# Seven quarter products for eight in one block product of a blocked token mixer

## The chip, the core and the metric

The kernel runs on one core of a Trainium2 chip. A core has five engines with queues of their own: TensorE (PE in the profile, its weight loads PEld), VectorE (DVE), ScalarE (ACT), GpSimd (POOL) and SyncE (SP), which mostly issues transfers. The metric is the device time of one execution in microseconds. Lower is better.

## The reference, cut to what matters

```python
x = x + A(layernorm(x), wqkv, wo)                        # 32 heads of 18, a query sees 8 keys, 2 apart
x = x + B(layernorm(x), w_in, w_sp, b_sp, w_out)
x = x + A(...); x = x + B(...)                           # the same weights again

def B(x, w_in, w_sp, b_sp, w_out):                       # S=2048 tokens, D=576, Fh=2304
    z = gelu(x @ w_in)                                   # 2048 x 4608
    z1, z2 = z[:, :Fh], layernorm(z[:, Fh:])
    g = w_sp @ z2 + b_sp[:, None]                        # 2048 x 2048 times 2048 x 2304
    return (z1 * g) @ w_out
```

The change concerns `w_sp @ z2`, the largest product of the program. It is computed twice, once for each B.

## The kernel before

The program has five phases: an attention stage (`phase_F(0)`, which also computes z2), a mixing stage (`phase_S(1)`), the same two again (`phase_F(2)`, `phase_S(3)`), and a last stage with the product by `w_out` (`phase_E`). In the attention stages a planner (`Flow`) orders the steps of all engines ahead of time. Each step has a cost, a key, the steps that it comes after and the buffers that it holds; the planner plays the engines forward and writes the instructions in the order that comes out. A step's cost on POOL or SP therefore takes part in the order of everything behind it. The constants of this play are in `PLANS`. `SIDE` names the queue of the stage's side transfers: POOL at 0.66 us in the first attention stage, SP in the second. `win2.0` to `win2.9` load a part of `w_in` on it, each after the logits step `a3.L` to `a12.L` of a tile of queries.

In a mixing stage the order is written out by hand. The stage has 18 units: nine feature tiles `jj` (each 2 x 128 features, s = 0 and 1) for each half `c` of the 2048 target tokens, numbered n = 0 to 17, the first half first. A unit multiplies 2 x 128 features by 2048 source tokens and 1024 target tokens. The operands are split in two in each dimension: z2 into B[b, s] (source half b, feature half s), w_sp into A11, A12, A21 and A22 (target block, source half). The product of two such 2 x 2 block matrices is taken with seven block products and sums for the usual eight:

- `A11`: B[0,0] with A11, into PSUM bank y
- `A12`: B[1,0] with A12, into bank x
- `S1`, `S2`, `S4`, `S3`: B or the sums T1 to T3 with S1 to S4, sums of the blocks of w_sp, into banks v and y
- `A22`: T4 with A22, into bank y

Each is eight matmuls of 128 x 128 by 128 x 512 (`eight`, L1281). Bank y alternates between two banks from unit to unit; x and v are one bank each. After each group VectorE evicts the bank (`plus`, L1303: scale, add the bias or an earlier part) into one of three buffers g0 to g2 and multiplies finished blocks by z1 (`times_u`, L1293). For A12 that is an eviction that adds g0, and a product. The T sums of the next unit (`t_op`, L1289) are made as soon as the present unit has used theirs. Between S3 and the end the unit also takes the z1 product of the next unit (`z1_a`, `z1_b`, 20 matmuls, L1254 and L1262), which ScalarE evicts with the GELU (L1266).

The sums of w_sp for the first half are made at the end of the first attention stage, and those for the second half in the first mixing stage: a transposing DMA brings a piece, ScalarE scales it (L1417), VectorE makes its sums (L1424), POOL stores it. That goes on beside units 2 to 7, at places named in a table. In unit 8 the blocks of the second half are loaded over those of the first. In the second mixing stage both halves come from DRAM.

The query, key and value weights lie in SBUF for the whole program in five tiles: `wqk`, `wqk_r` and `wqk_e` (query and key, in an order that the first stage makes with VectorE, POOL and ScalarE copies), `wv` and `wv_r` (value). Both attention stages read them, no mixing stage does.

Of the kernel before, what the change touches and what calls it, by code (L numbers as in the profile page):

```python
# [46 lines left out]
ORDER = ("A11", "A12", "S1", "S2", "S4", "S3", "A22")  # L47
PLACED = ("A11", "A12", "S1", "S2", "S4", "S3", "A22")
BLOCKS = ("A11", "A12", "A22", "S3", "S1", "S2", "S4")

# [218 lines left out]
class K:  # L269
# [17 lines left out]
    def setup(self):  # L287
        nc, tc, ctx = self.nc, self.tc, self.ctx
        c = self.base = ctx.enter_context(tc.tile_pool(name="base", bufs=1))
        self.dram = ctx.enter_context(tc.tile_pool(name="dram", bufs=1, space=DRAM))  # L290
        self.xres = [self.dram.tile([S, D], bf16, name=f"xres{i}") for i in range(2)]
        self.psum = ctx.enter_context(tc.tile_pool(name="ps", bufs=1, space=PSUM)).tile([P, 8, 512], f32, name="psum")
        self.flow, self.turn, self.pair_at = None, [0, 0], (0, 1, 2, 3)
        self.xnD = c.tile([P, NM + 1, 2080], bf16, name="xnD")[:, :, 16 - PADL:16 - PADL + XW]
        self.ident = c.tile([P, P], bf16, name="ident")
        self.maskT = c.tile([P, QH], bf16, name="maskT")
        self.mask0 = c.tile([P, QH], bf16, name="mask0")
        self.zu = c.tile([P, NZ, 2 * S], bf16, name="zu")
        self.wA = c.tile([P, WA * 2, D], bf16, name="wA")
        self.wqk = c.tile([P, NM, NM, 2, P], bf16, name="wqk")  # L300
        self.wqk_r = c.tile([P, NM, P], bf16, name="wqk_r")
        self.wqk_e = c.tile([P, NM + 1, P], bf16, name="wqk_e")
        self.wv = c.tile([P, NM, 2, 2, 144], bf16, name="wv")
        self.wv_r = c.tile([P, 2, 2, 144], bf16, name="wv_r")
        self.wsc = c.tile([P, 8], f32, name="wsc")
        self.neg_half = self.wsc[:, 7:8]
        self.ustore = [self.dram.tile([P, S], bf16, name=f"ustore{j}") for j in range(NB)]
        self.ops = {(k, n): self.dram.tile([P, 8 * 512], f16 if n[0] == "S" else bf16, name=f"op{k}_{n}")
                    for k in range(1) for n in BLOCKS}
        self.ops1 = self.dram.tile([P, len(BLOCKS), 8 * 512], bf16, name="op1")  # L310
        self.first_pairs, self.blk = None, {}
        make_identity(nc, self.ident[:])
        self.idle = self.zu[:, NB, 0:512]
        nc.vector.memset(self.idle, 0.0)
        nc.vector.memset(self.neg_half, -0.5)
        self.xn_writes, self.xn_strided = [], []
        self.wrote_xn(nc.vector.memset(self.xnD[:, :, 0:PADL], 0.0), 0, PADL)
        self.wrote_xn(nc.vector.memset(self.xnD[:, :, PADL + S:XW], 0.0), PADL + S, XW)
# [212 lines left out]
    def phase_F(self, li):  # L531
# [550 lines left out]
        for i in range(NS):  # L1082
            Z2_steps(i, pl.KZ + pl.KS * i, [f"win2.{k}" for k in range(len(win2_parts()))] +
                     ([] if first else [f"p3_{j}.m11" for j in range(NS)]))
        fl.step("blocks", "SP", 0.0, 900, lambda _: self.open_blocks(li + 1, acm), [f"w{i}.m1" for i in range(NS)])
        (self.make_ops if first else self.load_first_ops)(fl)
        self.flow = fl
# [113 lines left out]
    def phase_S(self, li):  # L1201
# [27 lines left out]
        def bias(c, a):  # L1229
            return bsp[:, b_of[c, a], :]  # L1230
# [48 lines left out]
        def eight(ps, lhs, rhs, opens):  # L1279
            for i in range(8):  # L1280
                nc.tensor.matmul(ps, lhsT=lhs[:, i, :], rhs=rhs[:, i, :], start=(opens and i == 0), stop=(i == 7),  # L1281
                                 skip_group_check=not opens)
            self.pairs += 8

        def t_op(jj, k):

            B = z_of(jj)
            a, b = {1: (B[0, 1], B[0, 0]), 2: (B[1, 1], T[0][:]), 3: (B[1, 1], B[0, 1]), 4: (B[1, 0], T[1][:])}[k]
            nc.vector.tensor_tensor(out=T[k - 1][:], in0=a, in1=b, op=ALU.subtract)  # L1289

        def times_u(u, a, s, g):
            uv = u[:, s, 512 * a:512 * a + 512]
            nc.vector.tensor_tensor(out=uv, in0=g, in1=uv, op=ALU.mult)  # L1293

        def unit(n, jj, c, z1, t_next, at):
            B, u = z_of(jj), u_of(jj, c)
            y = self.psum[:, Y.start + n % 2, :]
            x, v = self.psum[:, XV.start, :], self.psum[:, XV.start + 1, :]
            g0, g1, g2 = (t[:] for t in tmp)
            h0, h1, h2 = (t[:].bitcast(bf16)[:, 0:512] for t in tmp)  # L1300

            def plus(out, ps, other):
                nc.vector.scalar_tensor_tensor(out=out, in0=ps, scalar=inv[c], in1=other, op0=ALU.mult, op1=ALU.add)  # L1303

            def t_one(k):
                if t_next is not None:
                    t_op(t_next, k)
            at("begin")
            eight(y, B[0, 0], A["A11"], True)
            at("A11")  # L1310
            plus(g0, y, bias(c, 0))
            at("first")
            eight(x, B[1, 0], A["A12"], True)
            at("A12")
            plus(h1, x, g0)
            times_u(u, 0, 0, h1)
            eight(v, T[0], A["S1"], True)
            at("S1")
            plus(g1, v, bias(c, 1))
            at("third")  # L1320
            t_one(1)
            eight(y, T[1], A["S2"], False)
            at("S2")
            plus(g2, y, bias(c, 0))
            t_one(2)
            eight(v, B[1, 1], A["S4"], False)
            at("S4")
            plus(h0, v, g2)
            times_u(u, 0, 1, h0)
            eight(y, T[2], A["S3"], False)  # L1330
            at("S3")
            plus(h2, y, g1)
            times_u(u, 1, 1, h2)
            if z1:
                z1_a(*z1, ZB)
            t_one(3)
            at("second")
            eight(y, T[3], A["A22"], False)
            at("A22")
            plus(h0, y, bias(c, 1))  # L1340
            times_u(u, 1, 0, h0)
            t_one(4)
            if z1:
                z1_b(*z1, ZB)
            at("end")
# [87 lines left out]
                piece_load(i + 2)  # L1433

        seq = [(jj, c) for c in range(2) for jj in range(NB)]
        for n, (jj, c) in enumerate(seq):
            nxt = seq[n + 1] if n + 1 < len(seq) else None
            z1 = nxt
            if n + 2 < len(seq):
                load_w1(*seq[n + 2])  # L1440

            def at(where, n=n, jj=jj, c=c):
                if first and n < 2:
                    first_sums(n, where)
                for part, k in pieces.get((n, where), ()):
                    if part == 0:
                        piece_scale(k)
                    else:
                        piece_sums(k, part - 1)
                    if part == 2:  # L1450
                        piece_store(k)
                if where == "S3":
# [16 lines left out]
            unit(n, jj, c, z1, nxt[0] if nxt else None, at)  # L1469
            if c == 0:  # L1470
                spill(jj)
        order.__exit__(None, None, None)
# [86 lines left out]
```

## Time and profile before

| | |
|---|---|
| median of 3 runs | 1132.14 us (1129.98 to 1133.3) |
| profiled execution | 1129.72 us, its span 1128.0 us |
| granted TensorE clock | 0.997 |
| busy share of the span | PE 98%, DVE 63%, ACT 38%, POOL 19% |
| first mixing stage, first z1 matmul | 201.9 us |
| first matmul of unit 0, of unit 1 | 206.0 and 229.2 us |
| second attention stage, first matmul | 500.1 us |
| second mixing stage, first z1 matmul | 761.8 us |
| last stage | about 1052 to 1128 us |

The profile is of one execution, 2.4 us below the median of the runs. Times count from the start of the span. A row names engine, line, operation, output and inputs, shape and number, then the time busy and the mean of one; behind the bar or in brackets stands how long the engine was idle before, and what ended that. Matmuls are pipelined, so the mean of one (381 ns for 512 columns) is its latency and not the spacing of two.

### The profile page before, as it was taken

The numbers are of one execution on the slowest core, as the hardware profiler recorded it, in microseconds if no ns is written. First come the engines' busy times: TensorE is split into PE (matmuls) and PEld (weight loads), VectorE is DVE, ScalarE is ACT, GpSimd is POOL, SyncE is SP. The second block draws the span as 40 slices with busy tenths as digits, with TensorE's granted clock in tenths as the row PEclk, the third lists the DMA queues.
The fourth block names the chain that finished last, engine by engine and source line by source line (L and its number), as shares of the span: only waits on it lengthen the run. The fifth ranks groups of instructions, "written<-read, shape, count | busy, mean of one in ns | idle before, by whom it ended". The sixth has DMA issues, their size and how long they took to land. (4 is left out here: it accounts for less than half of the span.)

```text
span 1128.0 us, 24364 instructions
## 1 busy us (share of the span) xinstructions
PE 1103.6 (98%) x10109; PEld 612.2 (54%) x10147; DVE 712.4 (63%) x1205; ACT 431.2 (38%) x684; POOL 217.3 (19%) x436
## 2 busy tenths in 40 slices
PE   8999999899999999999999999999999999999998
PEld 5777655344444444457777765554444444444676
DVE  8898888866765555554566777556555555555311
ACT  7788897642221101103454668772101110111000
POOL 6353538302110000022111214520000000000000
PEclk9999999999999999999999999999999999999999
DMA  7866460658967331133444777602112383221221
GB/s 191 166 141 134 104 138 1 176 165 243 247 215 283 117 117 42 46 108 95 73 70 73 122 164 185 203 1 56 49 40 59 85 311 88 72 56 38 85 64 53
DMA packets 187528, 131.82 MB, mean 117 GB/s; under 512 B 145273, under 2 KB 171769, under 8 KB 183833
## 3 DMA queue, kind: packets, MB, share of 16 engines
q1 hardware_dynamic: 179032, 96.54, 35.2%
q0 software_dynamic: 8384, 33.72, 9.2%
q8 instruction: 79, 1.29, 0.5%
q14 instruction: 33, 0.26, 0.1%
HBM read 68.40 MB, written 31.20 MB: 88 GB/s over the span
## 5 line engine op out<-in xcount | busy, mean ns | idle before, releaser
L1266 ACT ACTIVATE zu<-psum 128x1024 bf16<-128x1024 f32 x72 | 73.5, 1023 | 436.3 <-PE psum L1262 386.9
L1303 DVE SCALAR_TENSOR_TENSOR g<-psum,wsc,bsp 128x512 f32<-128x512 f32 (+1 forms) x144 | 108.0, 750 | 154.2 <-PE psum L1281 153.8
L1281 PE MATMUL psum<-S,T 128*128 128x512 f16 x864 | 199.9, 381 | 0.2 <-DVE T L1289 0.2
L1281 PEld LDWEIGHTS <-T 128*128 128x128 f16 x1152 | 113.0, 98 | 138.9 <-issue 4.3
L1281 PEld LDWEIGHTS <-zu 128*128 128x128 bf16 x864 | 84.5, 98 | 107.8 <-DVE zu L964 3.8
L1254 PE MATMUL psum<-xnD,w 128*128 128x512 bf16 x540 | 134.5, 380 | 1.9
L1281 PE MATMUL psum<-A,zu 128*128 128x512 bf16 x576 | 130.7, 379 | 2.7 <-DVE zu L964 2.7
L481 PEld LDWEIGHTS <-zu 128*128 128x128 bf16 x1152 | 112.5, 98 | 29.3 <-issue 0.2
L1303 DVE SCALAR_TENSOR_TENSOR g<-psum,wsc,g 128x512 bf16<-128x512 f32 x108 | 81.1, 751 | 62.5 <-PE psum L1281 62.1
L900 PE MATMUL psum<-wA,xnD 128*128 128x384 bf16 x576 | 109.7, 327 | 0.3 <-DVE v_ext L461 0.3
L481 PE MATMUL psum<-wA,zu 128*128 128x288 bf16 x768 | 105.0, 286 | 0.0
L900 PEld LDWEIGHTS <-xnD 128*128 128x128 bf16 x768 | 72.0, 98 | 56.2 <-issue 12.2
L1254 PEld LDWEIGHTS <-w 128*128 128x128 bf16 x576 | 53.4, 98 | 74.3 <-issue 15.3
L923 ACT ACTIVATE zu<-psum 128x768 bf16<-128x768 f32 x96 | 76.8, 804 | 22.7 <-PE psum L907 17.4
L933 DVE CUSTOM_DVE_ANT_1 zu<-zu 128x1536 bf16<-128x1536 bf16 x32 | 56.0, 1751 | 29.1 <-ACT zu L923 28.8
L1281 PE MATMUL psum<-S,zu 128*128 128x512 f16 x288 | 68.0, 379 | 2.1 <-DVE g L1303 2.1
L1281 PE MATMUL psum<-A,T 128*128 128x512 bf16 x286 | 67.9, 379 | 1.5 <-DVE g L1303 1.4
L786 ACT ACTIVATE P<-psum 128x912 bf16<-128x912 f32 x72 | 64.0, 944 | 9.5 <-PE psum L779 7.7
L1293 DVE TENSOR_TENSOR zu<-g,zu 128x512 bf16<-128x512 bf16 x144 | 61.2, 425 | 10.0 <-DVE g L1303 0.9
L391 PE MATMUL psum<-xnD,wqk 128*128 128x228 bf16 (+1 forms) x480 | 64.9, 280 | 2.4 <-ACT xnD L462 1.2
L391 PEld LDWEIGHTS <-wqk 128*128 128x128 bf16 x480 | 43.8, 97 | 16.9 <-issue 7.6
L427 ACT ACTIVATE xn<-xt,ln_st 128x512 bf16<-128x512 bf16 x72 | 42.9, 647 | 20.4 <-POOL ln_st L414 20.3
(151 smaller groups left out, 1336.3 us busy)
## 6 DMA issues: line engine op xcount, KB each, us to landing
w<-in_B_w_in_dram SPq DMA_DIRECT2D x72, 128.0 KB
ustore<-zu POOLq DMA_DIRECT2D x18, 512.0 KB, 3.6
zu<-ustore SPq DMA_DIRECT2D x18, 512.0 KB
S<-op SPq DMA_DIRECT2D x8, 1024.0 KB
A<-op SPq DMA_DIRECT2D x6, 1024.0 KB
QK<-stg SPq DMA_DIRECT2D x36, 114.0 KB
QK<-stg SPq DMA_DIRECT2D x24, 171.0 KB
wA<-in_B_w_sp_dram POOLq DMA_DIRECT2D x8, 512.0 KB, 4.8
```

The costliest lines, as they stand in the source:

```text
L391: nc.tensor.matmul(ps(s), lhsT=lhsT, rhs=rhs, start=(c == 0 and not rest_first), stop=(c == NM - 1 and rest_first))
L427: nc.scalar.activation(out=out, in_=in_, func=ACT.Identity, scale=rstd[:n], bias=nmr[:n])
L481: nc.tensor.matmul(ps[:, hh, 0:288], lhsT=u[:, s * S + i * P:s * S + (i + 1) * P], rhs=wout(b, s)[:, hh * 288:(hh + 1) * 288], start=(b == ...
L786: nc.scalar.activation(out=Psb[:, 2 * hh:2 * hh + 2, :, 0:QH], in_=box["L", hh][:, :, 0:8 * QH].rearrange("p a (b c) -> p a b c", c=QH), f ...
L900: nc.tensor.matmul(box[u][:, s, 0:384], lhsT=self.xnD[:, c, at], rhs=(win2a[:, c, s] if c < NM - 1 else win2b[:, s])[:, cols], start=(firs ...
L923: nc.scalar.activation(out=self.zu[:, 3 * u:3 * u + 3, 256 * i:256 * (i + 1)].rearrange("p j (s r) -> p s j r", s=2), in_=box[u][:, :, 0:3 ...
L933: nc.vector.tensor_tensor_reduce(out=junk(0, 6), in0=z[:, 0:6, :], in1=z[:, 0:6, :], scale=1.0 / FH, scalar=0.0, op0=ALU.mult, op1=ALU.add ...
L1254: nc.tensor.matmul(ps[:, h, :], lhsT=w1[:, NM * h + d, :], rhs=self.xnD[:, d, t0:t0 + 512], start=(opens and d == 0), stop=(not opens and ...
L1266: nc.scalar.activation(out=u_of(jj, c)[:, :, 512 * k:512 * k + 512], in_=ps, func=ACT.Gelu_apprx_tanh)
L1281: nc.tensor.matmul(ps, lhsT=lhs[:, i, :], rhs=rhs[:, i, :], start=(opens and i == 0), stop=(i == 7), skip_group_check=not opens)
L1293: nc.vector.tensor_tensor(out=uv, in0=g, in1=uv, op=ALU.mult)
L1303: nc.vector.scalar_tensor_tensor(out=out, in0=ps, scalar=inv[c], in1=other, op0=ALU.mult, op1=ALU.add)
```

## The change

Units 2 and 3, 4 and 5, 6 and 7 of the first half, and the tiles 0 and 1, 2 and 3, 4 and 5, 6 and 7 of the second, form pairs. For a pair the product of B[1,0] with A12 is taken for both tiles together, in the first unit of the pair (kind "two"). Seen as one product it has 2 x 128 features (one 128 from each tile), 1024 source tokens and 512 target tokens, and is again split in two in each dimension: seven quarter products of four matmuls of 128 x 128 by 128 x 256 (`four`), where two times eight matmuls of 512 columns stood. The part that belongs to the second tile is kept in f32 (`late`), and the second unit (kind "parked") has no A12 group: it adds `late` to its A11 and multiplies by z1 at once. Tile 8 of each half and units 0 and 1 (kind "one") stay as they were.

The sums that the quarters need are SQ (four of 128 x 1024, from A12, made once for each half by `s_quarter`) and TQ (four of 128 x 512, from the z2 of both tiles, made by `t_quarter` in the unit before the pair, between S3 and A22). SQ, TQ, `late` and the finished block `hq` lie in the space of the query, key and value weights, which become one tile `wqkv` with five parts. In the first attention stage four stores on POOL's queue (`keep0` to `keep3`, after the logits of tiles 13 to 16) copy it to DRAM, and at the start of unit 17 of the first mixing stage one load on SP's queue brings it back. After the second attention stage it is not needed any more.

```diff
+WQ = (0, 4096, 4608, 5248, 7552, 8128)
...
+        self.wqkv = c.tile([P, WQ[-1]], bf16, name="wqkv")
+        part = [self.wqkv[:, WQ[k]:WQ[k + 1]] for k in range(5)]
...
+        self.wqkv_d = self.dram.tile([P, WQ[-1]], bf16, name="wqkv_d")
...
+            for k in range(4):
+                fl.step(f"keep{k}", *SIDE, 0, lambda _, k=k: self.dma(self.wqkv_d[:, 2032 * k:2032 * k + 2032], self.wqkv[:, 2032 * k:2032 * k + 2032], side),
+                        made + [f"a{13 + k}.L"])
...
+        def s_quarter(k):
+            to, x, y, op = ((SQ[0], quarter(1, 0), quarter(1, 1), ALU.add), (SQ[2], quarter(0, 0), quarter(1, 0), ALU.subtract),
+                            (SQ[1], SQ[0], quarter(0, 0), ALU.subtract), (SQ[3], quarter(0, 1), SQ[1], ALU.subtract))[k]
+            nc.vector.tensor_tensor(out=to, in0=x, in1=y, op=op)
...
+        def t_quarter(jj):
+            B = z_quarters(jj)
+            for k, a, b in ((0, B[0, 1], B[0, 0]), (1, B[1, 1], TQ[0]), (2, B[1, 1], B[0, 1]), (3, B[1, 0], TQ[1])):
+                nc.vector.tensor_tensor(out=TQ[k], in0=a, in1=b, op=ALU.subtract)
+
+        def four(ps, lhs, rhs, opens):
+            for i in range(4):
+                nc.tensor.matmul(ps, lhsT=lhs[:, i, :], rhs=rhs[:, i, :], start=(opens and i == 0), stop=(i == 3),
+                                 skip_group_check=not opens)
...
             at("A11")
-            plus(g0, y, bias(c, 0))
+            if kind == "parked":
+                plus(h1, y, late)
+                times_u(u, 0, 0, h1)
+            else:
+                plus(g0, y, bias(c, 0))
             at("first")
-            eight(x, B[1, 0], A["A12"], True)
+            if kind == "one":
+                eight(x, B[1, 0], A["A12"], True)
+            if kind == "two":
+                four(yq, Q[0, 0], quarter(0, 0), True)
             at("A12")
...
+            if kind == "two":
+                plus(g0[:, half(0)], yq, g0[:, half(0)])
             eight(v, T[0], A["S1"], True)
             at("S1")
             plus(g1, v, bias(c, 1))
             at("third")
             t_one(1)
+            if kind == "two":
+                four(xq, Q[1, 0], quarter(0, 1), True)
+                plus(hq[:, half(0)], xq, g0[:, half(0)])
             eight(y, T[1], A["S2"], False)
             at("S2")
             plus(g2, y, bias(c, 0))
             t_one(2)
+            if kind == "two":
+                four(xq, TQ[0], SQ[0], True)
+                plus(late[:, half(1)], xq, bias(c, 0)[:, half(1)])
+                four(yq, TQ[1], SQ[1], False)
+                plus(late[:, half(0)], yq, bias(c, 0)[:, half(0)])
             eight(v, B[1, 1], A["S4"], False)
             at("S4")
             plus(h0, v, g2)
             times_u(u, 0, 1, h0)
+            if kind == "two":
+                four(xq, Q[1, 1], SQ[3], False)
+                plus(late[:, half(0)], xq, late[:, half(0)])
+                four(yq, TQ[2], SQ[2], False)
+                plus(late[:, half(1)], yq, late[:, half(1)])
             eight(y, T[2], A["S3"], False)
             at("S3")
             plus(h2, y, g1)
             times_u(u, 1, 1, h2)
+            if kind == "two":
+                four(yq, TQ[3], quarter(1, 1), False)
+                plus(hq[:, half(1)], yq, g0[:, half(1)])
+                times_u(u, 0, 0, hq)
...
+            return "one" if jj == NB - 1 or n < 2 else "parked" if jj % 2 else "two"
...
+                if where == "second" and n + 1 < len(seq) and kind(n + 1) == "two":
+                    t_quarter(seq[n + 1][0])
...
+                if where == "begin" and n == len(seq) - 1 and first:
+                    self.dma(self.wqkv[:], self.wqkv_d[:])
```

`xq` is the first 256 columns of bank x, and `yq` those of the y bank that the unit itself does not use. `s_quarter` runs in units 1 and 2 for the first half and in unit 9 for the second.

More of the change, by code (lines that the diff above doesn't have):

```diff
@@ L299, in setup @@
         self.wA = c.tile([P, WA * 2, D], bf16, name="wA")
[L300 to L304, printed above, removed]
+        self.wqkv = c.tile([P, WQ[-1]], bf16, name="wqkv")
+        part = [self.wqkv[:, WQ[k]:WQ[k + 1]] for k in range(5)]
+        self.wqk = part[0].rearrange("p (b c s n) -> p b c s n", b=NM, c=NM, s=2)
+        self.wqk_r = part[1].rearrange("p (b n) -> p b n", b=NM)
+        self.wqk_e = part[2].rearrange("p (b n) -> p b n", b=NM + 1)
+        self.wv = part[3].rearrange("p (c b s n) -> p c b s n", c=NM, b=2, s=2)
+        self.wv_r = part[4].rearrange("p (b s n) -> p b s n", b=2, s=2)
+        self.wqkv_d = self.dram.tile([P, WQ[-1]], bf16, name="wqkv_d")
         self.wsc = c.tile([P, 8], f32, name="wsc")
@@ L1084, in phase_F @@
                      ([] if first else [f"p3_{j}.m11" for j in range(NS)]))
+        if first:
+            made = [f"wqk{b}" for b in range(NM)] + [f"ends{k}" for k in range(4)] + ["wqk_r", "wv"]
+            for k in range(4):
+                fl.step(f"keep{k}", *SIDE, 0, lambda _, k=k: self.dma(self.wqkv_d[:, 2032 * k:2032 * k + 2032], self.wqkv[:, 2032 * k:2032 * k + 2032], side),
+                        made + [f"a{13 + k}.L"])
         fl.step("blocks", "SP", 0.0, 900, lambda _: self.open_blocks(li + 1, acm), [f"w{i}.m1" for i in range(NS)])
@@ L1293, in times_u, with quarter, z_quarters, unit @@
             nc.vector.tensor_tensor(out=uv, in0=g, in1=uv, op=ALU.mult)
-        def unit(n, jj, c, z1, t_next, at):
+        fine = [self.wqkv[:, k:k + n].bitcast(f16).rearrange("p (i t) -> p i t", i=4)
+                for k, n in [(1024 * k, 1024) for k in range(4)] + [(4096 + 512 * k, 512) for k in range(4)]]
+        SQ, TQ = fine[0:4], fine[4:8]
+        late, hq = self.wqkv[:, 6144:7168].bitcast(f32), self.wqkv[:, 7168:7680]
+        xq = self.psum[:, XV.start, 0:256]
+        def quarter(a, b):
+            return A["A12"][:, 4 * b:4 * b + 4, 256 * a:256 * a + 256]
+        def s_quarter(k):
+            to, x, y, op = ((SQ[0], quarter(1, 0), quarter(1, 1), ALU.add), (SQ[2], quarter(0, 0), quarter(1, 0), ALU.subtract),
+                            (SQ[1], SQ[0], quarter(0, 0), ALU.subtract), (SQ[3], quarter(0, 1), SQ[1], ALU.subtract))[k]
+            nc.vector.tensor_tensor(out=to, in0=x, in1=y, op=op)
+        def z_quarters(jj):
+            return {(b, s): z_of(jj + s)[1, 0][:, 4 * b:4 * b + 4] for b in range(2) for s in range(2)}
+        def t_quarter(jj):
[6 more added lines that the diff above has]
+                                 skip_group_check=not opens)
+            self.pairs += 4
+        def unit(n, jj, c, z1, t_next, kind, at):
             B, u = z_of(jj), u_of(jj, c)
+            Q = z_quarters(jj) if kind == "two" else None
+            yq = self.psum[:, Y.start + (n + 1) % 2, 0:256]
             y = self.psum[:, Y.start + n % 2, :]
@@ L1307, in t_one, with half @@
                     t_op(t_next, k)
+            def half(k):
+                return slice(256 * k, 256 * k + 256)
             at("begin")
@@ L1310, in unit @@
             at("A11")
-            plus(g0, y, bias(c, 0))
+            if kind == "parked":
[3 more added lines that the diff above has]
+                plus(g0, y, bias(c, 0))
             at("first")
-            eight(x, B[1, 0], A["A12"], True)
+            if kind == "one":
+                eight(x, B[1, 0], A["A12"], True)
+            if kind == "two":
+                four(yq, Q[0, 0], quarter(0, 0), True)
             at("A12")
-            plus(h1, x, g0)
-            times_u(u, 0, 0, h1)
+            if kind == "one":
+                plus(h1, x, g0)
+                times_u(u, 0, 0, h1)
+            if kind == "two":
+                plus(g0[:, half(0)], yq, g0[:, half(0)])
             eight(v, T[0], A["S1"], True)
@@ L1435, in phase_S, with kind @@
         seq = [(jj, c) for c in range(2) for jj in range(NB)]
+        def kind(n):
+            jj = n % NB
+            return "one" if jj == NB - 1 or n < 2 else "parked" if jj % 2 else "two"
         for n, (jj, c) in enumerate(seq):
@@ L1451, in at @@
                         piece_store(k)
+                if where == "second" and n + 1 < len(seq) and kind(n + 1) == "two":
+                    t_quarter(seq[n + 1][0])
+                for k in range(4):
+                    if (n % NB, where) == (((1, "begin"), (1, "A11"), (1, "end"), (2, "A11")) if n < NB else
+                                           ((0, "begin"), (0, "A11"), (0, "first"), (0, "S1")))[k]:
+                        s_quarter(k)
+                if where == "begin" and n == len(seq) - 1 and first:
+                    self.dma(self.wqkv[:], self.wqkv_d[:])
                 if where == "S3":
@@ L1467, in at @@
                         self.load_wout(self.wA[:], 0, WA, nc.sync)
-            unit(n, jj, c, z1, nxt[0] if nxt else None, at)
+            unit(n, jj, c, z1, nxt[0] if nxt else None, kind(n), at)
             if c == 0:
```

## The prediction

> **What bounds the kernel now.** I read the page first, then the chain of work that ended last, then the waits and the timeline of the two mixing stages.
>
> ```profile
> span 1128.0 us, 24364 instructions
> PE 1103.6 (98%) x10109; PEld 612.2 (54%) x10147; DVE 712.4 (63%) x1205; ACT 431.2 (38%) x684; POOL 217.3 (19%) x436
> ...
> 782.96 10.36 PE psum L1281 x48
> 793.59 1.46 PE psum L1254 x6
> 795.04 1.73 PE psum L1281 x8
> 796.77 0.54 PE psum L1262 x4
> 797.31 1.83 PE psum L1254 x8
> 799.14 10.36 PE psum L1281 x48
> ...
> 1054.98 69.72 PE psum L481 x569
> ```
>
> PE is busy 98% of the span. The second fence part is the chain in order of time: start, length, what. One unit of a mixing stage is 56 block matmuls (L1281) and 20 z1 matmuls; its period is 799.14 - 782.96 = 16.18 us, and the chain never leaves PE in it. So a matmul taken out of a unit is worth its pace, as long as nothing else gets late. The pace at 512 columns is 10.36/48 = 215.8 ns; at 288 columns (each with new weights, as here) 69.72/569 = 122.5 ns.
>
> ```profile
> PE psum L1281 <- DVE g L1303: 2.9, 2, 1.5
> ...
> PE psum L1281 <- DVE g L1303: 0.6, 1, 0.6
> ```
>
> These are all of PE's waits from 217 to 500 us and from 765 to 1060 us (total, times, longest). Nearly every one of the 36 units runs without a wait.
>
> **The products.** A pair of tiles takes A12 today as 2 x 8 matmuls of 512 columns, 16 x 0.2158 = 3.45 us. Afterwards it takes 7 x 4 matmuls of 256 columns. No 256-wide matmul stands in the trace; the rows on both sides bound it:
>
> ```profile
> 56.42 0.68 PEld L391 LDWEIGHTS <-wqk 128*128 128x128 bf16 x7 [0.31 <-issue]
> L391 PEld LDWEIGHTS <-wqk 128*128 128x128 bf16 x480 | 43.8, 97 | 16.9 <-issue 7.6
> ```
>
> Seven weight loads, one per 228-column matmul, first start to last end 0.68 us: (0.68 - 0.097)/6 = 97 ns each. A straight line from 97 at 228 columns to 122.5 at 288 gives 109 at 256, and the loads keep up with the shorter matmul at 228. So 28 x 0.109 = 3.05 us and a pair gains 0.40. The ends are 97 (gain 0.74) and 122.5 (gain 0.02); I take 0.40, since 97, 122.5 and 215.8 lie on nearly one line, 0.42 ns a column. The break-even is 3.45/28 = 123 ns.
>
> "two" holds for tiles 2, 4, 6 in the first half and 0, 2, 4, 6 in the second: 7 pairs per stage, 14 in all. 14 x 0.40 = 5.6 us less on PE.
>
> A rule of the Trainium skill speaks against this (TensorE: Matmul & The Clock Gate, Back-to-back issue gap): a sustained stream is said to take about 81 ns a matmul at 128 columns and 131 at 512. A line through those, an estimate, gives 98 at 256, and a pair would go from 16 x 131 = 2.10 us to 28 x 98 = 2.74, a loss. The 215.8 ns above disagree with its 131, and the measurement decides.
>
> **Does VectorE follow?** A "two" unit gets seven 256-wide evictions for one of 512, its neighbour loses one, and that neighbour computes four half-size sums.
>
> ```profile
> 886.80 1.89 PE L1281 MATMUL psum<-S,zu 128*128 128x512 f16 x8
> 887.00 0.75 DVE L1303 SCALAR_TENSOR_TENSOR g<-psum,wsc,bsp 128x512 f32<-128x512 f32 x1 [0.38 <-PE psum L1281]
> 887.67 0.68 DVE L1289 TENSOR_TENSOR T<-zu,T 128x1024 f16<-128x1024 bf16 x1
> ...
> L1293 DVE TENSOR_TENSOR zu<-g,zu 128x512 bf16<-128x512 bf16 x144 | 61.2, 425 | 10.0 <-DVE g L1303 0.9
> L461 DVE CAST stg<-psum 128x684 bf16<-128x684 f32 x15 | 13.1, 871 | 10.5 <-PE psum L391 8.4 <-PE psum L385 2.1
> L461 DVE CAST stg<-psum 128x456 bf16<-128x456 f32 x13 | 8.2, 627 | 1.0 <-PE psum L385 0.5 <-PE psum L391 0.3
> ...
> 772.72 0.76 DVE g L1303
> 773.52 3.61 PE psum L1281 x16
> ```
>
> An eviction starts 0.20 us after its group's last issue (887.00 against 886.80); the next independent operation starts 0.67 after a 0.75 one; PE goes on 0.04 after the eviction that it waits for (773.48 to 773.52). From PSUM an element costs (871 - 627)/228 = 1.07 ns, so 256 columns fewer take 0.27 off 0.75: 0.48 us. A half-size sum has 512 elements, 0.425 us.
>
> From the start of a "two" unit, PE's order gives: S1 issued by 3.89, first quarter on x by 4.33, S2 by 6.05, two quarters, S4 by 8.65, two quarters, S3 by 11.25, last quarter. Two reuses of a bank are tight. The third quarter overwrites x at 6.05: g1 starts at 4.09, T1 at 4.76, the quarter's eviction at 5.36, done 5.84, free 5.88: 0.17 to spare. The last quarter adds to y at 11.25: h0 at 8.85, its product 9.69, two evictions at 10.03 and 10.43, done 10.91, free 10.95: 0.30 to spare. In the neighbour the four half-size sums lie in the idle time before A22. So steady pairs wait for nothing. The bounds for a pair are 0 and 0.36 (below, first rival). The unit lengths become 17.5 and 14.45 us for 2 x 16.18.
>
> **Units with other work in the first stage.** There VectorE also makes the sums for the other half of w_sp, piece by piece.
>
> ```profile
> 252.36 0.75 DVE L1424 TENSOR_TENSOR wA<-wA 128x512 f16<-128x512 bf16 x2
> ...
> 271.63 2.00 ACT L1417 ACTIVATE wA<-wA,wsc 128x2048 bf16<-128x2048 bf16 x1 [8.75 <-DMA wA<-in_B_w_sp_dram]
> 273.66 0.88 DVE L1424 TENSOR_TENSOR wA<-wA 128x512 f16<-128x512 bf16 x2 [1.97 <-ACT wA L1417]
> 275.26 1.89 PE L1281 MATMUL psum<-A,T 128*128 128x512 bf16 x8 [1.36 <-DVE g L1303]
> ...
> 327.90 3.62 PE L1281 MATMUL psum<-A,zu 128*128 128x512 bf16 x16
> ...
> 329.07 1.99 ACT L1417 ACTIVATE wA<-wA,wsc 128x2048 bf16<-128x2048 bf16 x1
> ```
>
> The 1.36 us wait of unit 3 ends a chain that a transposing DMA sets: piece 0's last sums, their store, piece 2's load, its scaling, its sums, h2. After the change unit 3's S3 comes 0.4 earlier, and the chain's first sums (unit start + 6.89 now) about 1.1 earlier, since they no longer queue behind a late g1. So this wait becomes 0.7 if the chain moves and 1.8 if not; I leave it at 1.36. In unit 7 the scaling ends 3.16 us into the unit (331.06 against 327.90); four sums of 0.38 take VectorE to 4.7, g1 to 5.45, and without A12 S4 wants v at 5.18: 0.3 lost. In unit 6 two such sums push the last quarter's eviction by 0.4 where 0.30 was to spare: 0.1 lost. Together 0.4 lost, bounds 0.7 gained and 1.1 lost.
>
> **The weights in DRAM.** Reload: 128 x 8128 x 2 bytes = 2.08 MB on SP's queue.
>
> ```profile
> 481.52 0.56 SPq L285 DMA_DIRECT2D zu<-ustore  x1
> 496.84 0.89 SPq L285 DMA_DIRECT2D wB<-in_B_w_out_dram  x2
> 528.43 1.32 PE L391 MATMUL psum<-xnD,wqk 128*128 128x342 bf16 x8
> ...
> DMA to landing us min/median/max: 6.8/7.9/9.1
> ```
>
> The last line is for the 1 MB block loads; two of them bound this one by 14 to 18 us. It issues behind the u reload at 482.1, and SP has nothing until 496.84; the first user runs at 528.43. Queued behind it is the load of w_out's last rows. Cost 0; without that cover up to 3 us.
>
> Save: four stores of 0.52 MB on POOL's queue in the first attention stage, after tile 12's logits.
>
> ```profile
> 93.81 0.62 POOL L285 DMA_DIRECT2D wC<-in_B_w_in_dram  x1 [0.18 <-issue]
> ustore<-zu POOLq DMA_DIRECT2D x18, 512.0 KB, 3.6
> 80.00:100.00 20.00, 20.00 (x471) 15.74 (x469) 17.48 (x37) 18.47 (x29) 11.39 (x23) 1.00 0.75 149
> 100.00:120.00 20.00, 19.68 (x471) 14.70 (x469) 17.45 (x32) 14.69 (x24) 5.47 (x10) 1.00 0.51 99
> 505.00:765.00 260.00, 253.33 (x3566) 169.10 (x3566) 165.02 (x284) 160.48 (x285) 71.30 (x167) 0.99 0.51 111
> ...
> 205.96 2.97 PE L1281 MATMUL psum<-A,zu 128*128 128x512 bf16 x13
> 213.05 5.31 PE L1281 MATMUL psum<-S,T 128*128 128x512 f16 x16 [0.20 <-DVE T L1289]
> 229.15 3.62 PE L1281 MATMUL psum<-A,zu 128*128 128x512 bf16 x16
> ```
>
> In the window rows stand the busy times of PE, PEld, DVE, ACT and POOL, the granted clock, the DMA share and GB/s. 93.81 is the last of the stage's ten weight loads on that queue, so the stores follow from there to about 115 us, 0.6 us of POOL and 3.6 us of transfer each. POOL is 27 to 57% busy there (11.39 and 5.47 of 20), DMA 0.75 and 0.51, PE full. By themselves they are hidden: queued behind them on POOL are layer-norm scalars and row stores whose readers come tens of us later. But the planner counts POOL's time, so the order of everything after them can come out otherwise. I put 0 for that. The bounds: 1.7 gained (the 16 matmuls at 213.05 take 5.31 us for 3.6, a loss that another order may not have), 9.3 lost (last rival).
>
> **The sum.** 5.6 - 0.4 = 5.2 us less. The profiled execution took 1129.72 us (span 1128.0), so it becomes 1124.5; the median of the runs, 1132.14, lies 2.4 above it, so I predict 1126.9, 0.46% less. A measurement tells about 0.3% (3.4 us) from no change here.
>
> **Rivals.**
> *VectorE becomes the bound.* If a 256-wide eviction costs the 0.75 us of the full one, the third quarter waits 0.10 us and the last one 0.25: 0.35 of 0.40 gone in each pair, 0.7 us left, given back by the first stage's 0.4. Time 1131.8: no change. For it: the margins of 0.17 and 0.30. Against: the slope of 1.07 ns. Chance 0.14.
> *Matmuls pay a fixed price.* Were the 97 ns weight load not hidden beside a 256-wide matmul, each would take 206 ns, a pair 5.77 us and the stages 14 x 2.32 = 32 more: 1165. The 228-column row speaks against it; it decides from 123 ns. The skill's rule above would end here, at 14 x 0.64 = 9 us more. Chance 0.02.
> *One tile for all weights.* If accesses to the shared tile were ordered as a whole and not by region, each quarter would wait for the eviction before it, over 1 us at each of some four places a pair: 50 us more, 1180. Against: the z buffer is one tile too, read by PE and written by VectorE and ScalarE side by side. Chance 0.04.
> *The first stage is planned worse* (the slower side). The second attention stage, with other constants, leaves PE 260 - 253.33 = 6.7 us idle, 2.6%; the first leaves 0.32 in 40. At 2.6% over its last 100 us it would lose 2.3. The handover to unit 0 (205.96 to 229.15, 23.2 us for 16.18) costs 7.0 us now; the same again if the last norms come later. Together 9.3: 1136.2, 4 us slower. It decides from 5.2 + 3.4 = 8.6 us. For it: the handover already hangs on VectorE and POOL. Against: the stores come 90 us earlier. Chance 0.14, and 0.06 for a milder form that loses 2 to 5 us: 1130.4, no change.
>
> **The numbers.** The forecast keeps 0.60, all of it faster by over 0.3%. No change: 0.14 + 0.06 = 0.20. Slower: 0.14 + 0.04 + 0.02 = 0.20. The range leaves out these last three. Low: 1126.9 less 1.7 and 0.7 and the runs' own 1.5, 1123.0. High: the VectorE case with the same spread and the piece chain not moving, 1134.0. The forecast's own range is 1123.0 to 1129.0.
>
> **What would show it.** Unit periods of 17.5 and 14.45 us; four quarter matmuls in 0.44 us; evictions of 256 columns at 0.48 us; no PE wait in steady pairs, and about 1.4 us in unit 3; the reload landed by 500 us with the query products at their place; unit 0 of the first stage as long as now. Wrong it is if quarter groups start late behind L1303, or if the first attention stage or its handover is longer by more than 2 us.

## The result and the profile after

The kernel after takes 1120.62 us (median of 4 runs, 1119.61 to 1124.71), the kernel before on the same chip 1132.22 (4 runs). The ratio is 0.9907, 95% interval 0.9878 to 0.9936. The forecast had 1126.9 with a range of 1123.0 to 1134.0: the sign was right, the gain is 11.6 us where 5.2 was forecast, and the range misses it. The profiled execution took 1119.61 us.

The page of the kernel after, first its span and the row of busy times:

```profile
span 1117.9 us, 24828 instructions
PE 1094.8 (98%) x10277; PEld 627.9 (56%) x10315; DVE 760.5 (68%) x1345; ACT 431.5 (39%) x686; POOL 219.4 (20%) x440
```

PE is still the bound at 98%, and VectorE's 48 us more cost nothing that the share shows. The chain of work that ended last, over a pair of tiles in the second mixing stage (start, length, what; L1290 was L1281, L1328 is `four`, L1263 was L1254):

```profile
793.60 0.44 PE psum L1328 x4
794.03 1.73 PE psum L1290 x8
795.76 0.44 PE psum L1328 x4
796.19 1.73 PE psum L1290 x8
797.92 0.87 PE psum L1328 x8
798.79 1.73 PE psum L1290 x8
800.52 0.87 PE psum L1328 x8
801.39 1.73 PE psum L1290 x8
803.12 0.44 PE psum L1328 x4
...
809.38 8.63 PE psum L1290 x40
```

The seven quarters take 0.44 + 0.44 + 0.87 + 0.87 + 0.44 = 3.06 us, 109 ns a matmul, in the place of 3.45. The 40 in one piece at 809.38 are a "parked" unit. PE's waits in the two mixing stages, 217 to 500 and 765 to 1060 us:

```profile
PE psum L1290 <- DVE g L1342: 3.2, 1, 3.2
PE psum L1328 <- DVE wqkv L1342: 1.1, 1, 1.1
...
PE psum L1290 <- DVE g L1342: 0.2, 1, 0.2
```

The 3.2 us lie in unit 0 of the first stage, whose length did not change. The 1.1 are in unit 4, of which more below. No steady pair waits. Where the time went is read from the starts of four units, here the rows of the timeline for unit 17 of the first mixing stage and units 0 and 17 of the second, before, and then for units 1, 17, 0 and 17 after (unit 1 before, at 229.15, stands in the prediction):

```profile
489.74 0.59 PE L1281 MATMUL psum<-A,zu 128*128 128x512 bf16 x2
765.88 0.59 PE L1281 MATMUL psum<-A,zu 128*128 128x512 bf16 x2
1041.73 0.59 PE L1281 MATMUL psum<-A,zu 128*128 128x512 bf16 x2
```

```profile
229.31 0.59 PE L1290 MATMUL psum<-A,zu 128*128 128x512 bf16 x2
487.19 0.59 PE L1290 MATMUL psum<-A,zu 128*128 128x512 bf16 x2
758.98 0.59 PE L1290 MATMUL psum<-A,zu 128*128 128x512 bf16 x2
1031.68 0.59 PE L1290 MATMUL psum<-A,zu 128*128 128x512 bf16 x2
```

| stretch | before | after | difference |
|---|---|---|---|
| start to unit 1, first mixing stage | 229.15 | 229.31 | +0.16 |
| its units 1 to 17 | 260.59 | 257.88 | -2.71 |
| unit 17 to unit 0 of the second (this holds the second attention stage) | 276.14 | 271.79 | **-4.35** |
| units 0 to 17 of the second mixing stage | 275.85 | 272.70 | -3.15 |
| the rest | 86.27 | 86.22 | -0.05 |

The 5.9 us in the two mixing stages are close to the 5.2 that the change was counted at. The 4.35 in a stage whose work the change does not touch were not foreseen. Here is the window of 505 to 765 us, which the prediction showed of the kernel before, of the kernel after (PE, PEld, DVE, ACT, POOL, clock, DMA share, GB/s), and the waits of PE in it:

```profile
505.00:765.00 260.00, 255.66 (x3577) 169.53 (x3577) 170.30 (x292) 161.64 (x288) 69.64 (x161) 1.00 0.47 110
```

```profile
PE psum L805 <- ACT P L790: 0.9, 1, 0.9
PE psum L783 <- DVE xt L530: 0.9, 1, 0.9
...
PE psum L871 <- ACT oT L466: 0.4, 1, 0.4
```

and before, over 490 to 765 us:

```profile
PE psum L867 <- ACT oT L462: 2.1, 2, 1.7
PE psum L779 <- ACT P L786: 0.9, 2, 0.5
```

PE idles 2.3 us less in the window, and the longest wait of before, 1.7 us for `oT`, has shrunk to 0.4. Behind that wait the trace of before has one thing more, in its rows of single microseconds (PE's busy time, granted clock, DMA share, GB/s):

```profile
668.00:669.00 1.00, 0.04 (x1) 1.00 1.57 290
669.00:670.00 1.00, 0.28 (x3) 1.00 0.89 188
670.00:671.00 1.00, 1.00 (x39) 1.00 1.03 260
671.00:672.00 1.00, 1.00 (x20) 0.62 0.00 0
672.00:673.00 1.00, 1.00 (x12) 0.50 0.09 16
673.00:674.00 1.00, 1.00 (x8) 0.50 0.90 127
674.00:675.00 1.00, 1.00 (x8) 0.67 0.29 37
```

PE idles for 1.7 us; 1.5 us after it is back the clock is granted at half for a stretch. The shortfalls 0.38 + 0.50 + 0.50 + 0.33 add to 1.7 us lost. With the 2.3 us of idle time this makes 4.0 of the 4.35. The profile of after has no such stretch anywhere: its clock is 1.000 over the span, that of before 0.997. The trace of before has a second one, at 213.85 us in unit 0 of the first mixing stage. It cost no time: its 16 matmuls took 5.31 us, those of after take 3.63, and both units last 23.19 us, since PE then waits longer for VectorE (3.2 us for 1.5).

### The profile page after: what moved, and what is told of

It is laid out like the page before. It is cut to its first block, busy times and chain, and to the rows that moved or that the text cites. A ratio compares the mean times of both kernels' runs of the same rounds, so it can differ in the third digit from the quotient of the medians.

```text
span 1117.9 us, 24828 instructions
## 1 busy us (share of the span) xinstructions
PE 1094.8 (98%) x10277; PEld 627.9 (56%) x10315; DVE 760.5 (68%) x1345; ACT 431.5 (39%) x686; POOL 219.4 (20%) x440
## 3 DMA queue, kind: packets, MB, share of 16 engines
q8 instruction: 80, 1.31, 0.5%
## 5 line engine op out<-in xcount | busy, mean ns | idle before, releaser
L1290 PE MATMUL psum<-S,T 128*128 128x512 f16 x864 | 200.5, 379 | 0.2 <-DVE T L1298 0.2
L1290 PEld LDWEIGHTS <-T 128*128 128x128 f16 x1152 | 112.7, 98 | 127.1 <-DVE T L1298 0.5
L1342 DVE SCALAR_TENSOR_TENSOR g<-psum,wsc,bsp 128x512 f32<-128x512 f32 (+1 forms) x130 | 97.5, 750 | 95.3 <-PE psum L1290 93.8
L1263 PE MATMUL psum<-xnD,w 128*128 128x512 bf16 x540 | 134.5, 380 | 1.9
L485 PEld LDWEIGHTS <-zu 128*128 128x128 bf16 x1152 | 112.5, 98 | 29.3
L1290 PEld LDWEIGHTS <-zu 128*128 128x128 bf16 x640 | 62.6, 98 | 80.0 <-issue 4.4
L1263 PEld LDWEIGHTS <-w 128*128 128x128 bf16 x576 | 53.4, 98 | 71.3 <-issue 15.3
L1342 DVE SCALAR_TENSOR_TENSOR g<-psum,wsc,g 128x512 bf16<-128x512 f32 (+1 forms) x94 | 66.8, 711 | 39.2 <-PE psum L1290 37.3
L1290 PE MATMUL psum<-A,zu 128*128 128x512 bf16 x352 | 82.4, 379 | 2.7 <-DVE zu L968 2.7
L1290 PE MATMUL psum<-S,zu 128*128 128x512 f16 x288 | 68.0, 379 | 3.5 <-DVE g L1342 3.4
L1290 PE MATMUL psum<-A,T 128*128 128x512 bf16 x286 | 67.9, 379 | 0.1
L395 PE MATMUL psum<-xnD,wqkv 128*128 128x228 bf16 (+1 forms) x480 | 64.9, 280 | 2.0 <-ACT xnD L466 1.2
L1302 DVE TENSOR_TENSOR zu<-g,zu 128x512 bf16<-128x512 bf16 x130 | 55.3, 425 | 9.0 <-DVE g L1342 0.4
L395 PEld LDWEIGHTS <-wqkv 128*128 128x128 bf16 x480 | 43.7, 97 | 16.5 <-issue 7.6
L530 DVE TENSOR_TENSOR ob<-psum,x 128x576 bf16<-128x576 f32 (+1 forms) x17 | 12.3, 722 | 56.7 <-PE psum L485 56.7
```

Of the source, the lines that this page charges most:

```text
L395: nc.tensor.matmul(ps(s), lhsT=lhsT, rhs=rhs, start=(c == 0 and not rest_first), stop=(c == NM - 1 and rest_first))
L485: nc.tensor.matmul(ps[:, hh, 0:288], lhsT=u[:, s * S + i * P:s * S + (i + 1) * P], rhs=wout(b, s)[:, hh * 288:(hh + 1) * 288], start=(b == ...
L1263: nc.tensor.matmul(ps[:, h, :], lhsT=w1[:, NM * h + d, :], rhs=self.xnD[:, d, t0:t0 + 512], start=(opens and d == 0), stop=(not opens and ...
```

## The experiments

**Theory.** The planner puts the second attention stage in another order. It keeps a count of the matmuls written so far and models the code of PE as arriving in blocks of 128 pairs of weight load and matmul:

```python
BLOCK, PLACE, AHEAD, CROWD, HOLD = 128, 80, 146, 1.5, (0.6, 0.8)
...
a = self.pairs - self.PLACE - ahead
return [(k, (self.BLOCK * k - a) * rate) for k in range(a // self.BLOCK + 1, (a + st["pairs"]) // self.BLOCK + 1)]
```

`four` adds 4 to the count. A pair of tiles goes from 16 matmuls to 28, so the first mixing stage writes 7 x 12 = 84 more, and the second attention stage is planned with a count 84 higher. Written out by the kernel's own planner, the first attention stage and the last stage come in the order of before, while 108 of the 237 PE steps of the second attention stage stand elsewhere. The planner's own figure for the stage falls from 259.88 to 258.05 us. **Rivals:** the parking or the single weight tile changed the transfers of that stage; or the gain there was chance.

**The order put back, and the order alone.** Both edits touch only the count that the planner of the second attention stage is told; all matmuls stay.

```diff
-  ... pl.STAY, self.pairs, pl.LF,
+  ... pl.STAY, self.pairs if first else self.pairs - 84, pl.LF,     # e1, in the kernel after
+  ... pl.STAY, self.pairs if first else self.pairs + 84, pl.LF,     # e2, in the kernel before
```

> The changed kernel, with the planner of the second attention stage told 84 matmul pairs less, so that its order is that of before; its code still lies 84 pairs further on. Theory O (the order that the planner makes from the count of pairs gave 4.3 us of the gain): from unit 17 of the first mixing stage to unit 0 of the second 276.1 us, as before, and the time 1120.6 + 4.3 = 1124.9 us. Rival C (the place of the code, not the order): 271.8 us for that stretch, 1120.6. Rival P (the one weight tile and its reload): 271.8 and 1120.6 too.

> The kernel before, with the planner of the second attention stage told 84 matmul pairs more, so that its order is that of the changed kernel; products, weights and the place of the code are those of before. Theory O: the stretch from unit 17 to unit 0 takes 271.8 us instead of 276.1, and the time is 1132.2 - 4.3 = 1127.9 us. Rivals C and P: 276.1 and 1132.2.

e1 took 1125.99 us (12 runs) against 1130.14 for before, ratio 0.997 (0.9955 to 0.9985). e2 took 1127.12 (12 runs), ratio 0.9974 (0.996 to 0.9987). Both orders move the time the expected way, but the stretch from unit 17 to unit 0 took 280.95 us in e1 where 276.1 was expected, and 274.53 in e2 for 271.8. e1 has a wait in it that neither kernel has, the first of these rows, and the wait for `oT` of the kernel before is longer in it:

```profile
PE psum L783 <- issue: 3.0, 2, 1.9
PE psum L871 <- ACT oT L466: 2.6, 1, 2.6
```

In the first row PE stood still for no other engine. The order was planned for another place in the code than it has, so a block of code that is not there yet is the reading that fits. The packets of the instruction queue in the trace bear it out: one of 16 KB landed at 584.07 and one at 680.66 us, and PE went on 1.5 and 1.3 us later, at 585.54 and 681.95. These 3.0 us, and one half-clock stretch more than with the old order at its place (e5, below), make up the 4.7 us that e1 is over it. So these two are not clean, and the order has to be changed together with the true count.

**The old products with everything else.** The kernel after with all units "one" and without its sums; the one weight tile, the stores and the reload stay.

```diff
-            return "one" if jj == NB - 1 or n < 2 else "parked" if jj % 2 else "two"
+            return "one"
```

> The changed kernel with every unit of the kind one: eight whole products per pair as before, no SQ and TQ sums, but one weight tile, its stores and its reload. The count of pairs and the planner's order are those of before. Theory O and rival C: 1132.2 us, 276.1 us from unit 17 to unit 0. Rival P: 1127.9 and 271.8.

1130.17 us (12 runs), ratio 0.9996 (0.9981 to 1.0011). Parking the weights in DRAM and the single tile neither cost nor gain anything that can be measured, which here means more than about 2 us. As the cause of 4.35 us that rival is gone. The kernel after without the four stores and the reload (e3) gave no time, so what these cost apart from the single tile is not shown.

**Order and place together.** Tiny matmuls, their results overwritten, are written into unit 0 of the first mixing stage, half ahead of A12 and half ahead of S4, and counted. 44 of them in the kernel after make 84 + 44 = 128, a whole block, so that the old order comes out and fits its place in the code. 84 in the kernel before give the new order at its right place.

```diff
+        def filler(k, ps):
+            for _ in range(k):
+                nc.tensor.matmul(ps[0:32, 0:64], lhsT=self.ident[:, 0:32], rhs=self.ident[:, 0:64], start=True, stop=True)
+            self.pairs += k
...
+            if first and n == 0:
+                filler(22, v)        # e5, in the kernel after: 22 + 22; e6, in the kernel before: 42 + 42
```

> The changed kernel with 44 tiny matmuls (32 x 64 outputs, read by nobody) in the idle of unit 0 of the first mixing stage. 84 + 44 = 128 pairs is one whole block of code, so the second attention stage gets the order of before, planned for where its code really lies. Theory M (the order counts, and with it that the plan knows where the code lies: e1 had the old order and a plan 84 pairs off): what is left of the gain is that of the products, 5.9 us off 1130.1, 1124.2, and the stretch from unit 17 to unit 0 takes 276.1 us without waits for code. Theory O alone (the order, whatever lies where): as e1, 1126.0. Rival C (any shift of the code helps): as the changed kernel, 1119.6 by its ratio.

> The kernel before with 84 of the same tiny matmuls in the idle of unit 0: the order of the changed kernel in the second attention stage, planned for where its code lies, and no quarter product. Theory M: 1130.1 - 4.3 = 1125.8 us, the stretch 271.8. Theory O alone: as e2, 1127.1. Neither: 1130.1 or, if the tiny matmuls cost time, up to 3 us more.

> The changed kernel itself, beside the other two on one chip. All theories: 0.9907 of before, 1119.6 us where before takes 1130.1. With e5 and e6 it tells whether the two gains add up: 5.9 and 4.3 make 10.2.

On one chip, before 1130.52 (14 runs): e5 1123.24 (5 runs), ratio 0.9935 (0.9916 to 0.9953); e6 1126.08 (8 runs), 0.9957 (0.9941 to 0.9974); the kernel after 1122.67 (6 runs), 0.9933 (0.9914 to 0.9952). The first matmuls of unit 17 and of unit 0, of e5 and then e6:

```profile
487.18 0.59 PE L1290 MATMUL psum<-A,zu 128*128 128x512 bf16 x2
763.38 0.59 PE L1290 MATMUL psum<-A,zu 128*128 128x512 bf16 x2
```

```profile
489.33 0.59 PE L1281 MATMUL psum<-A,zu 128*128 128x512 bf16 x2
761.58 0.59 PE L1281 MATMUL psum<-A,zu 128*128 128x512 bf16 x2
```

The old order takes 276.20 us, as in the kernel before (276.14); the new one 272.25, as in the kernel after (271.79). So the unforeseen gain in this stage goes with the order: with the order and 84 tiny matmuls the kernel before gains 4.4 us. But 7.3 and 4.4 make 11.7, which is what the first measurement of the kernel after gave and not the 7.85 of this one. Beside e5, the kernel after is only 0.57 us faster here, less than the intervals can tell apart. So with the new products in place, the times of this chip do not show what the order is worth. A difference that the profiles show is the half-clock stretches: here the profile of after has two, one in unit 0 of the first mixing stage (24.87 us long in place of 23.19) and one in the second attention stage (274.25 in place of 271.79).

**Does the time follow the planner's order for other counts too?** With 58 tiny matmuls in the kernel after the planner's figure for the stage is 256.40 us, with 99 it is 268.50, with 128 the order is that of the kernel after.

```diff
-                filler(22, v) ... filler(22, x)
+                filler(29, v) ... filler(29, x)        # e8; e9: 64 and 64; e10: 50 and 49
```

> The kernel after with 58 tiny matmuls (32 rows x 64 columns, results overwritten) in the first unit of the first mixing stage, 29 ahead of A12 and 29 ahead of S4. The planner then starts the second attention stage at another place in its blocks of 128 pairs, and plans 256.4 us for it in place of 258.05. Theory A (the stage's time follows the order that the planner picks for the pair count): its stretch from the last unit of the first mixing stage to the first of the second takes 270.1 us without a half-clock stretch and 272.6 with one (271.8 and 274.3 in the kernel after); with the 1.7 us of a half-clock stretch gone from the first mixing unit, whose gaps the tiny matmuls fill, the time is 2 to 3 us under the kernel after, about 1120. Theory B (the planner's own spans say nothing of the chip at this size, the order's part was chance): the time of the kernel after again, 1122.7, or up to 1 us more for the tiny matmuls.

> The kernel after with 128 tiny matmuls in the first unit of the first mixing stage (64 and 64), a whole block, so that the order of the second attention stage is exactly that of the kernel after. Theory A with half-clock stretches: if it is PE's gaps in the first mixing unit that bring on the half-clock stretch of 3.41 us there, this unit takes 23.2 us and not 24.9, and the time is 1.7 us under the kernel after wherever that has the stretch, so about 1121.0; the second attention stage stays at 271.8 to 274.3. Rival: the tiny matmuls lie on PE's path; 128 of 27 ns are 3.5 us, 1126.

> The kernel after with 99 tiny matmuls (50 and 49): for this place in the blocks the planner finds a poor order, 268.5 us in place of 258.05. Theory A: the stretch of the second attention stage takes 10 us more than in the kernel after, about 282 to 284, and the time is about 1131. Theory B: as the kernel after, 1122 to 1124.

> The kernel after once more, beside the three others on one chip. All theories: 1120.3 where no half-clock stretch falls on PE's path, 1122 with one and 1123.7 with two; 1122 expected.

On one chip, before 1130.18 (17 runs): **e8 1118.47** (4 runs), ratio 0.9897 (0.9884 to 0.991); e9 1122.84 (6 runs), 0.9934 (0.9919 to 0.9949); e10 1134.68 (10 runs), 1.0042 (1.0027 to 1.0058); the kernel after 1122.81 (6 runs), 0.9936 (0.992 to 0.9952). Units 17 and 0 of e8, then of e10:

```profile
486.19 0.59 PE L1290 MATMUL psum<-A,zu 128*128 128x512 bf16 x2
757.25 0.59 PE L1290 MATMUL psum<-A,zu 128*128 128x512 bf16 x2
```

```profile
486.63 0.59 PE L1290 MATMUL psum<-A,zu 128*128 128x512 bf16 x2
773.83 0.59 PE L1290 MATMUL psum<-A,zu 128*128 128x512 bf16 x2
```

The same matmuls in the stage, 271.06 us in one and 287.20 in the other, where 270.1 and 282 to 284 were forecast: e10 is slower than the kernel before, with all of the products' gain in it. e8 beats both kernels, and so a count that happens to suit the planner brings 4.3 us on top of the 7.4 of the change. e9 missed its 1121.0: its tiny matmuls bought nothing, unit 0 taking 23.79 us, and the half-clock stretch fell in the attention stage. With more of them than e8, it is no faster than the kernel after, so they are not what makes e8 fast. All profiles together, with the half-clock stretches inside this stage counted from the granted clock and 1.7 us taken off for each:

| order (planner's figure, us) | kernel | unit 17 to unit 0 | half-clock stretches | less 1.7 for each |
|---|---|---|---|---|
| 256.40 | e8 | 271.06 | 0 | 271.1 |
| 258.05 | after; e6 | 271.79; 272.25 | 0; 0 | 271.8; 272.3 |
| 258.05 | e7; e9; e11 | 274.25; 273.80; 275.26 | 1; 1; 1 | 272.6; 272.1; 273.6 |
| 259.88 | before; e4; e5 | 276.14; 275.14; 276.20 | 1; 1; 1 | 274.4; 273.4; 274.5 |
| 268.50 | e10 | 287.20 | 2 | 283.8 |

(e11 also waits 2.0 us for a load of `w_in`, the row below.) The last column rises with the planner's figure, about 2 us from the new order to the old one and 12 to the worst, though e8 and e10 have one profile each. e1 and e2 fit as well: less 1.7 for each of their two stretches and one, and less their waits for code (3.0 and 0.3), they take 274.5 us in the old order and 272.5 in the new. On top of the order come the half-clock stretches: one in every profile of the old order in the table, in three of five of the new one. These are too few to say that the order sets how often they come.

```profile
PE psum L783 <- DMA wA<-in_B_w_in_dram: 2.0, 1, 2.0
```

## Why the prediction was wrong, and where it was right

**The step that failed** is the planner's reaction. The prediction named it ("the planner counts POOL's time, so the order of everything after them can come out otherwise. I put 0 for that") and looked for it in the first attention stage, where the stores are. That stage came out in the same order, with unit 1 at 229.31 for 229.15. The order changed in the second one, through the count of matmuls, which the prediction did not consider: with the products of before, the new order took that stage from 276.1 to 272.3 us (e6), 1.7 of it a half-clock stretch that the kernel before had. Its bounds for a replanning, 1.7 gained and 9.3 lost, would have had to stand at the second attention stage, which waits 6.7 us and so has something to give. The real term was 4.35 us of gain in the first profile. The sum also had no term for half-clock stretches. It read the one in unit 0 of the kernel before as a loss that another order may not have (the 5.31 us for 3.6), and when it was gone nothing was gained.

**How the 11.6 us divide.** The products, measured with order and place as before (e5) against kernels with the old products that had no late piece: units 1 to 17 take 256.63 us in e5 and 259.07 in e2, and the second stage 272.72 against 275.83, in all 5.55. The wait of a piece in the first stage adds 0 to 1.5 us to one kernel or the other, by the execution. The order is about 2 us by itself. The rest of the first measurement is put down to half-clock stretches, by the clocks alone: three of its four runs of the kernel after had a clock of 1.000 (1119.61 to 1120.9 us), and none of the runs of before listed with e1 to e11 came above 0.998. At a clock of 0.997 the kernel after takes 1122.0 (four runs of e7) and the kernel before 1130.3 (three runs beside them). So on the later chips the gain is 7.4 to 7.9 us (1122.81 against 1130.18, 1122.67 against 1130.52). At such a gain the forecast would have missed by 2 to 3 us and not by 6, so a part of the miss is the luck of one measurement. Why the stretches came less often in the first measurement of the kernel after was not settled.

**The products: right.** 14 pairs at 0.40 were forecast, and a pair measures 3.45 - 3.06 = 0.39. The straight line from 97 ns at 228 columns to 122.5 at 288 gave the 109 ns at 256 that were measured. The Trainium skill's 81 and 131 ns (TensorE: Matmul & The Clock Gate, Back-to-back issue gap) would, by the estimate worked out from them, have made the change a loss of 0.64 us a pair; the trace does not agree with them.

**VectorE: right.** The rows of one kind of 256-wide eviction and of a half-size sum, by shape:

```profile
L1342 DVE SCALAR_TENSOR_TENSOR wqkv<-psum,wsc,g 128x256 bf16<-128x256 f32 x28 | 13.4, 478 | 0.0
L1324 DVE TENSOR_TENSOR wqkv<-zu 128x512 f16<-128x512 bf16 x28 | 11.7, 418 | 0.0
```

They take 0.478 us against 0.48 and 0.418 against 0.425. The margins of 0.17 and 0.30 us held: unit periods in the second stage are 17.51 and 14.46 us (17.5 and 14.45 forecast), and the rival in which VectorE becomes the bound did not come about.

**Units with other work: half right.** Unit 7 lost 0.29 us (0.3 forecast) and unit 6 0.05 (0.1). The wait of unit 3, left at 1.36, is gone; the piece chain now meets unit 4, in some executions only:

```profile
280.29 2.00 ACT L1485 ACTIVATE wA<-wA,wsc 128x2048 bf16<-128x2048 bf16 x1 [1.47 <-DVE g L1342]
...
282.33 0.89 DVE L1492 TENSOR_TENSOR wA<-wA 128x512 f16<-128x512 bf16 x2 [1.47 <-ACT wA L1485]
...
284.92 1.03 PE L1328 MATMUL psum<-wqkv 128*128 128x256 f16 x8 [1.11 <-DVE wqkv L1342]
```

VectorE stood behind a late scaling of the piece, then made its sums, and an eviction that a quarter needs came after them. e9 has this too (1.16 us); e1, e5, e7, e8, e10 and e11 do not, and unit 4 takes 17.51 us there.

**The weights in DRAM: right.** The reload issued at 479.63, and in the row of DMA below (tenths in 40 slices from 478 to 490 us) all transfers end by 487, ahead of the 500 that was forecast; e4 puts its cost and the single tile's at nothing that can be measured. The rivals of a fixed price per matmul and of a tile ordered as a whole are excluded by the 109 ns and by pairs without waits.

```profile
479.63 0.55 SPq L286 DMA_DIRECT2D wqkv<-wqkv_d  x1
```

```profile
DMA  0000000146999996959595969898950000000000
```

## What to carry to other kernels

Where the order of a stage is computed from a running count, an instruction added upstream can replan it, even with the stage itself untouched: compare the computed order of each stage before and after, and make the count match to measure an edit by itself. Such a count is also a knob, here worth 4.3 us between the kernel after and e8 (beside 7.4 for the change) and 16 us between e8 and e10, and an edit judged without turning it is judged with a random draw of it. When a stage idles, look at the clock behind the idle time as well as at the wait.

## What was not expected of the hardware

A gap of PE shorter than 2 us can cost twice. In the kernel before 1.68 us of waiting are followed by a stretch at half clock that loses 1.7 us more; in the kernel after a run of waits of 0.9 us and less is not, while in e7, in the same order, it is. Each such stretch in these traces lasts 3.41 us. The Trainium skill (TensorE: Matmul & The Clock Gate, What's actually happening) has the clock set by how busy PE was over free-running windows of about 3.4 us, halved after an idle one. That the same waits bring a stretch in one execution and not in another agrees with free-running windows. That the gap need not fill a window is what the rows here add; the condition itself was not tested by an experiment.

Fetching code seems to cost PE time: e1, its order planned for a place 84 matmuls off, waited 3.0 us in two pieces for no other engine, and e5, with the order at its place, did not. But e8, planned for its place, waited 1.1 us in the same way (its row is below) and e10 0.8, so a wrong place is not the whole condition. The second attention stages of these runs hold six such waits, in e1, e2, e8 and e10, and in each PE goes on 1.3 to 1.5 us after a 16 KB packet of code has landed. The Trainium skill (Runtime: NRT & Kernel Launch, Instruction fetch mechanics) gives blocks of 16 KiB and calls the crossing mostly hidden. The page of the kernel after agrees on the size, 1.31 MB in 80 packets, 16.4 KB each; the waits in e1 would be what is left where it is not hidden. No experiment measured a crossing by itself.

```profile
PE psum L783 <- issue: 1.1, 1, 1.1
```

```profile
q8 instruction: 80, 1.31, 0.5%
```
